# Pacing the input loads of a fused attention and mixer kernel, and putting later ones off behind its transposing transfers

## The chip, the cores and the metric

The kernel runs on one core of a Trainium2 chip. The metric is the device time of one execution in microseconds. Before the change the median of three runs is 305.8 us (305.24 to 306.14).

A core has a matrix engine (TensorE, PE in the profile, its weight loads PEld), a vector engine (VectorE, DVE), a scalar engine (ScalarE, ACT), GpSimd (POOL), and SyncE (SP), which here only issues transfers. Each takes its instructions in the order in which they were written, and they wait for each other through semaphores. Transfers run on 16 DMA engines that all issuers share.

## The reference

For each of 8 batches and 8 heads, attention over 576 positions with heads of 64, a causal mask, and a bias from the running sum of the positive part of `s`; the heads side by side make `x`, which goes through a token mixer and a channel mixer:

```python
scores = scale * np.matmul(q, k.transpose(0, 1, 3, 2))
cum = np.cumsum(np.maximum(s, 0.0), axis=-1)
bias = -(cum[:, :, :, None] - cum[:, :, None, :])
scores = np.where(causal, -1000000000.0, scores + np.minimum(bias, 0.0))
attn = softmax(scores)
x = (attn @ v).transpose(0, 2, 1, 3).reshape(B, S, H * D)
...
h = np.maximum(x.transpose(0, 2, 1) @ w_tok1, 0.0) @ w_tok2
u = x + h.transpose(0, 2, 1)
return u + np.maximum(u @ w_ch1, 0.0) @ w_ch2
```

Inputs and output are float32; `q`, `k` and `v` are 9.4 MB each.

## The kernel before

The kernel is written as a list of operations (`P.op`), each with its cost in microseconds on every engine that may run it, the buffers it reads and writes, a priority, and for transfers a duration. A planner (`Plan.run`, L106) plays the list through on a model of the five engines and of one transfer pipe, and the instructions are then emitted in the order of the planned starts. So a change of a cost, of a dependency, or of where a load stands in the list can move instructions on every engine. After `STEADY` = 50 us of planned time the planner adds a margin behind a transfer or ahead of a matmul. In planned gaps of TensorE in the first `WARM` = 45 us it puts filler matmuls of zeros (L1135).

Per batch the work is:

- Loads, issued by GpSimd, which converts q and k to bf16 on the way: `stage_qk(b, h)` loads k, then q, for a quad of four heads (L462) into one of five `qkn` buffers; `stage_v(b)` loads v in five pieces (L613) into one of two `vf` buffers and multiplies each piece by the exponential of the running sum (`merge_v`, L631, "merges") into `vp`, of which even and odd batches have one each. All loads are in one chain on GpSimd: each is issued behind the one before it (`after=chain[-1]`).
- `quad(b, h)` turns k and q on TensorE (L689) and copies them out of PSUM into `kT` and `qT` (L699 on ScalarE, L701 on VectorE). `pair` makes scores (L731), exponentials (L739, ScalarE), masks (L748, VectorE), attention times v (L802), and divides (L831, L835).
- `tok(b)`: token mixer (L899, L961) and the sum `u`. For batches from 2 on, `u` is turned into `uT` by transposing transfers that SyncE issues (L977), four or five slices per batch; batch parity decides between `uTa` and `uTb`.
- `chan(b)`: channel mixer, first matmuls from `uT` (L1017), second (L1042), sum (L1050), and the store by SyncE (L1055, L1058).

A guard also checks that q and k are small enough for the form used: `squares` (L647) sums their squares on ScalarE. For batches 0 and 1 this needs a second load of q and k, `stage_sq`, which stands behind all other loads in the list. The running sum of `s` is one scan on VectorE (L534, `cum`); from it come the weights of v through one exponential (L540) and a turn on TensorE (L560).

The order of the list before is: the first loads and the weights, v of batch 1, then for all batches from 2 to 7 `stage_qk(b, 0)`, `stage_v(b)`, `stage_qk(b, 4)`, then `stage_sq` for batches 0 and 1, then quads, `tok` and `chan` batch by batch. How far a load runs ahead is limited by its buffer alone, and by a dependency on the load eight before it (L456).

Of the kernel before, what the change touches and what calls it, by code (L numbers as in the profile page):

```python
# [11 lines left out]
ALU = mybir.AluOpType  # L12


SWITCH = 0.095
STEADY = 50.0
MARGIN = 0.5
# [37 lines left out]
class Plan:  # L55
# [11 lines left out]
    def op(self, alts, reads=(), writes=(), prio=0, dma=0.0, holds=(), after=None, mode=0, lock=False, alone=None):  # L67
        o = Op()
        o.alts = alts
        o.prio = prio  # L70
        o.dma = dma
        o.mode = mode
        o.lock = lock
        o.alone = alone
        o.idx = len(self.ops)
        o.deps = set()
        o.users = []
        o.bufs = []
        for k in list(reads) + list(writes) + list(holds):
            b = k[0] if isinstance(k, tuple) else k  # L80
            if isinstance(b, Buf) and b not in o.bufs:
                o.bufs.append(b)
                b.left += 1
        for k in reads:
            w = self.writer.get(k)
            if w is not None:
                o.deps.add(w)
        for k in writes:
            w = self.writer.get(k)
            if w is not None:  # L90
                o.deps.add(w)
            for r in self.readers.get(k, ()):
                o.deps.add(r)
        for k in reads:
            self.readers.setdefault(k, []).append(o)
        for k in writes:
            self.writer[k] = o
            self.readers[k] = []
        o.deps.discard(o)
        o.after = after  # L100
        if after is not None:
            o.deps.add(after)
        self.ops.append(o)
        return o

    def run(self, eps=0.03):  # L106
# [11 lines left out]
        for o in ops:  # L118
            if o.nd == 0:
                for e in o.alts:  # L120
                    cands[e].append(o)
        dma_free = 6.0
        mode = 0
        order = []

# [17 lines left out]
        while left:  # L143
            best = None
            for e in engines:
                lst = []
                tmin = None
                for o in cands[e]:
                    st = slot_time(o)
                    if st is None:  # L150
                        continue
                    est = max(etime[e] + (SWITCH if e == "PE" and o.mode != mode else 0.0), o.ready, st)
                    if o.lock and e in held:
                        est = max(est, held["POOL" if e == "DVE" else "DVE"])
                    if o.alone is not None and o.alone.eng != e:
                        est = max(est, o.alone.until)
                    lst.append((est, o))
                    if tmin is None or est < tmin:
                        tmin = est
                if tmin is None:  # L160
                    continue
                pick = None
                slack = eps + (SWITCH if e == "PE" else 0.0)
                for est, o in lst:
                    if est <= tmin + slack:
                        key = (o.prio, o.idx) if e in ("PE", "SP", "POOL") else (o.prio, o.ready, o.idx)
                        if e == "PE":
                            key = (mode and not o.mode, *key)
                        if pick is None or key < pick[0]:
                            pick = (key, est, o)  # L170
                if best is None or pick[1] < best[1]:
                    best = (e, pick[1], pick[2])
            if best is None:
                stuck = [(e, len(c)) for e, c in cands.items()]
                raise RuntimeError(f"plan is stuck: {left} left, {stuck}")
            e, est, o = best
            occ, lat, fn = o.alts[e]
            for b in o.bufs:
                if b.slot is None:
                    r = b.ring  # L180
                    i = min((i for i in range(len(r.tiles)) if not r.busy[i]), key=lambda i: r.free[i])
                    b.slot = i
                    b.begin = est
                    r.uses.append(b)
                    r.busy[i] = True
                    if b.ordered:
                        r.queue.pop(0)
            etime[e] = est + occ
            if o.alone is not None:
                o.alone.eng, o.alone.until = e, est + occ + 0.1  # L190
            if o.lock and e in held:
                held[e] = est + occ + 0.06
            if e == "PE":
                mode = o.mode
            if o.dma:
                s0 = max(est + (1.9 if e == "POOL" else 1.3), dma_free)
                dma_free = s0 + o.dma
                fin = dma_free + 0.9
            else:
                fin = est + lat  # L200
            o.start, o.fin, o.eng = est, fin, e
            for b in o.bufs:
                b.left -= 1
                b.end = max(b.end, fin)
                if b.left == 0:
                    b.ring.busy[b.slot] = False
                    b.ring.free[b.slot] = b.end
            for e2 in o.alts:
                cands[e2].remove(o)
            o.fn = fn  # L210
            order.append(o)
            for u in o.users:
                if u.after is o:
                    rdy = est + occ
                elif u.alts.keys() == {"PE"} and e == "PE":
                    rdy = est + occ
                elif e in u.alts and len(u.alts) == 1 and not o.dma:
                    rdy = est + occ
                else:
                    rdy = fin  # L220
                    if fin > STEADY:
                        rdy += MARGIN_DMA if o.dma else MARGIN if u.alts.keys() == {"PE"} else 0.0
                u.ready = max(u.ready, rdy)
                u.nd -= 1
                if u.nd == 0:
                    for e2 in u.alts:
                        cands[e2].append(u)
            left -= 1
# [139 lines left out]
def kernel(  # L368
# [34 lines left out]
    def sb(name, shape, dt, pool=None):  # L403
        return (pool or const).tile(shape, dt, name=name, tag=name)
# [44 lines left out]
    chain = []  # L449
    sent = []  # L450

    def load_op(fn, key, us, occ=0.75, prio=-1):

        o = P.op({"POOL": (occ, 0, fn)}, writes=key, prio=prio, dma=us, after=chain[-1] if chain else None)
        if len(sent) >= 8:
            o.deps.add(sent[-8])  # L456
        sent.append(o)
        chain.append(o)

    def load_cast(n, b, h, i, src):  # L460
        def load():
            nc.gpsimd.dma_start(  # L462
                out=n.t[:, i, :, :],
                in_=src[b, h : h + 4, :, :].rearrange("(f e) (p r) d -> (e p) f (r d)", e=2, r=R))
        load_op(load, [(n, i)], 1.45, prio=-1 if b or h else -3)

    qkn = {}

# [47 lines left out]
    for ti, src in enumerate((k, q)):  # L516
# [4 lines left out]
        for f in range(2):  # L521
# [9 lines left out]
         writes=["s"], prio=-7)  # L531
    P.op(dve(576, lambda: nc.vector.tensor_scalar_max(out=s_sb[:, :], in0=s_sb[:, :], scalar1=0.0)),
         reads=["s"], writes=["sr"], prio=-1)
    P.op({"DVE": (1.3, 1.6, lambda: nc.vector.tensor_tensor_scan(  # L534
        out=cum[:, :], data0=one_sb[:, :], data1=s_sb[:, :], initial=0.0, op0=ALU.mult, op1=ALU.add))},
        reads=["sr"], writes=["cum"], prio=-1)
    P.op(dve(1, lambda: nc.vector.tensor_scalar(
        out=half[:, :], in0=cum[:, S - 1 : S], scalar1=-0.5, scalar2=None, op0=ALU.mult)),
        reads=["cum"], writes=["half"], prio=-1)
# [59 lines left out]
    def stage_v(b, cs=tuple(range(NJ))):  # L599
# [4 lines left out]
        for c in cs:  # L604
# [10 lines left out]
            if b == 0 and c == NJ - 1:  # L615
                P.op({"SP": (0.6, 5.5, load_first)}, writes=[(vf, c)], prio=-2)
                continue
            load_op(load, [(vf, c)], 1.15 * n / 128, 0.92)
        if b:
            merge_v(b, cs)  # L620

# [41 lines left out]
    def stage_sq(b, h):  # L663
        n = Buf(r_qn)
        for i, src in enumerate((k, q)):
            load_cast(n, b, h, i, src)
        squares(b, h, n)
# [4 lines left out]
    def quad(b, h):  # L672
# [4 lines left out]
        for ti in range(2):  # L677
# [6 lines left out]
            def tr(ti=ti, pv=pv):  # L684
                for r in range(R):
                    for e in range(2):
                        p0 = e * PR
                        for f in range(2):
                            nc.tensor.transpose(out=pv(e)[f * D : f * D + D, r * PR : (r + 1) * PR],  # L689
                                                in_=nat.t[p0 : p0 + PR, ti, f, r * D : (r + 1) * D],  # L690
                                                identity=ident[p0 : p0 + PR, p0 : p0 + PR])
            P.op({"PE": (R * 0.031, R * 0.031 + 0.21, tr)}, reads=([(nat, ti, 0), (nat, ti, 1)] if b == 0 and h == 0 else [(nat, ti)]) + ["ident"] + pads,
                 writes=[(pts[e], e) for e in range(2)], holds=[d[ti] for d in dsts], prio=(np_ - 30 * (b < 1 and h < 1), 2), mode=1)
            for e in range(2):
                def ev(eng, ti=ti, e=e, pv=pv):
                    i = pv(e)[:, 0:S].rearrange("d (r p) -> d p r", r=R)
# [385 lines left out]
    for i in range(2, 4):  # L1082
        load_ch2(i)
    stage_v(1)
    for b in range(2, B):
        stage_qk(b, 0)
        stage_v(b)
        stage_qk(b, 4)
    for b in range(2):
        for h in range(0, H, 4):  # L1090
            stage_sq(b, h)
    for b in range(B):
        for h in range(0, H, 4):
            quad(b, h)
        st = tok(b)
        chan(b, *st)

    P.op({"DVE": (1.3, 1.6, lambda: nc.vector.tensor_tensor_scan(
        out=pre[:, :], data0=one_sb[:, :], data1=wn[:, 0:S], initial=0.0, op0=ALU.mult, op1=ALU.add))},
# [84 lines left out]
```

## Time and profile before

| | |
|---|---|
| median of 3 runs | 305.8 us (305.24 to 306.14) |
| the profiled execution's own time | 306.06 us |
| its span in the profile | 304.3 us |
| mean granted TensorE clock | 0.995 |
| loads by GpSimd (q0) | 24.25 MB, 44.6% of 16 engines' span |
| stores and transposes by SyncE (q1) | 14.44 MB, 18.7% |
| mean DMA rate over the span | 129 GB/s |

The span runs from the first to the last instruction that the profiler recorded; the profiled execution's own time has 1.76 us more around it. In a timeline row stand the start, the duration, engine, line, operation, output and inputs, shape, the number of instructions that were merged into the row, and in brackets the idle time ahead of it with what ended it. In the rows of 10 us stand the stretch, its length, then for PE, PEld, DVE, ACT and POOL the busy time and the number of instructions, the granted clock, the mean share of the DMA engines in use, and GB/s. A row of transfers has the issuing engine, the number, the size and the median time from issue to landing. "issue" is idle time for which the profile shows no cause.

### The profile page before, as it was taken

To read this page: it belongs to the slowest core of one execution; us is meant where nothing else is said; L and a number is where in the kernel's file an instruction comes from. 1 tells how busy PE (TensorE), PEld (TensorE's weight loads), DVE (VectorE), ACT (ScalarE), POOL (GpSimd) and SP (SyncE) were. 2 spreads that over 40 slices of the span, in tenths; PEclk is the share of its full clock that TensorE was granted. 3 is DMA by queue.
4 is the path that set the end of the run, shared out by engine and by line. 5 is a ranking of instruction groups with operands and counts; after the bars stand their busy time and mean duration, and the time that the engine had idled before them with its cause. 6 is when DMAs were issued, how large, how long until landed. Compare 5 with 4: busy or idle time off the path is not lost.

```text
span 304.3 us, 8094 instructions
## 1 busy us (share of the span) xinstructions
PE 291.8 (96%) x3430; PEld 168.2 (55%) x3430; DVE 172.0 (57%) x368; ACT 182.8 (60%) x298; POOL 107.6 (35%) x147
## 2 busy tenths in 40 slices
PE   8899999899999999999999999998999999999991
PEld 3478566467754545457754545455764544457550
DVE  5962889377976456756556556956456642420030
ACT  5887884699996486609872387727761286017300
POOL 8675469999780418107620108500000000000000
PEclk9999999999999999999999999999999999999998
DMA  8999999999997673358455535894004310250032
GB/s 218 226 207 206 216 224 229 252 190 262 227 156 125 155 197 54 79 140 178 94 80 103 133 84 83 132 116 136 2 2 84 125 38 0 69 155 2 0 111 74
DMA packets 38348, 39.29 MB, mean 129 GB/s; under 512 B 17600, under 2 KB 30976, under 8 KB 38304
## 3 DMA queue, kind: packets, MB, share of 16 engines
q0 software_dynamic: 17072, 24.25, 44.6%
q1 hardware_dynamic: 21232, 14.44, 18.7%
q8 instruction: 29, 0.48, 0.7%
q14 instruction: 15, 0.12, 0.1%
HBM read 40.65 MB, written 9.44 MB: 165 GB/s over the span
## 4 chain that ended last, share of the span: by engine, by line
PE 84%; DMA 12%; POOL 1%; issue 1%; DVE 0%; POOLq 0%
PE pmx L1017 30%; PE pmx L1042 30%; PE pmx L961 5%; PE pmx L899 5%; PE psc L802 5%; PE psc L731 5%; DMA qkn<-in_k_dram 5%; PE psc L689 3%; DMA wc<-in_moe_w_ch_dram 3%; DMA vf<-in_v_dram 2%; DMA uTb<-us 2%; POOL qkn L462 1%; PE pmx L986 0%; DVE of L1050 0%; POOL keep masks.py:66 0%
## 5 line engine op out<-in xcount | busy, mean ns | idle before, releaser
L1017 PEld LDWEIGHTS <-wc 128*128 128x128 bf16 x624 | 57.9, 98 | 32.6 <-issue 1.5
L739 ACT ACTIVATE E<-psc 128x1024 bf16<-128x1024 f32 x64 | 62.2, 1024 | 22.8 <-PE psc L731 22.2
L1017 PE MATMUL pmx<-uTb,wc 128*128 128x320 bf16 (+2 forms) x384 | 56.1, 299 | 1.4 <-DMA uTb<-ub 1.1
L1042 PE MATMUL pmx<-wc,gb 128*128 128x512 bf16 (+1 forms) x252 | 55.3, 369 | 0.0
L1017 PE MATMUL pmx<-uTa,wc 128*128 128x512 bf16 (+1 forms) x240 | 45.6, 337 | 0.0
L647 ACT ACTIVATE junk<-qkn 128x1152 bf16<-128x1152 bf16 x32 | 37.3, 1166 | 11.7 <-DMA qkn<-in_q_dram 11.3
L1042 PE MATMUL pmx<-wc,ga 128*128 128x512 bf16 x192 | 44.1, 379 | 0.0
L631 POOL TENSOR_TENSOR vp<-vf,wT 128x512 bf16<-128x512 f32 (+1 forms) x31 | 32.3, 1058 | 25.6 <-PE psc L802 24.9
L1024 ACT ACTIVATE gb<-pmx 128x320 bf16<-128x320 f32 (+2 forms) x57 | 24.7, 438 | 21.2 <-PE pmx L1017 17.3
L1042 PEld LDWEIGHTS <-gb 128*128 128x128 bf16 x252 | 23.6, 98 | 24.8 <-issue 0.2
L613 POOL DMA_DIRECT2D vf<-in_v_dram x39 | 34.1, 884 | 7.3 <-DMA qkn<-in_k_dram 2.2
L748 DVE TENSOR_TENSOR E<-E,keep 128x512 bf16<-128x512 bf16 x56 | 25.8, 474 | 13.3 <-ACT E L739 13.1
L1042 PEld LDWEIGHTS <-ga 128*128 128x128 bf16 x192 | 18.2, 98 | 20.4
L1024 ACT ACTIVATE ga<-pmx 128x512 bf16<-128x512 f32 (+1 forms) x36 | 19.2, 535 | 11.7 <-PE pmx L1017 11.1
L462 POOL DMA_DIRECT2D qkn<-in_k_dram x19 | 14.1, 744 | 33.5 <-issue 31.8
L1026 DVE TENSOR_SCALAR gb<-pmx 128x320 bf16<-128x320 f32 (+2 forms) x39 | 18.8, 487 | 11.9 <-PE pmx L1017 11.5
L699 ACT COPY kT<-psc 128x576 bf16<-128x576 bf16 x22 | 13.1, 641 | 19.4 <-PE psc L689 17.9
L802 PEld LDWEIGHTS <-E 128*128 128x128 bf16 x576 | 21.1, 97 | 5.5
L835 DVE TENSOR_TENSOR x<-psc,rc 128x640 bf16<-128x640 f32 x28 | 23.0, 823 | 0.9
L1050 DVE TENSOR_TENSOR of<-pmx,ua 128x512 f32<-128x512 f32 x16 | 11.0, 689 | 19.5 <-PE pmx L1042 19.3
L731 PE MATMUL psc<-qT,kT 64*128 64x256 bf16 (+2 forms) x320 | 21.3, 250 | 0.0
L731 PEld LDWEIGHTS <-kT 64*128 64x128 bf16 x320 | 12.6, 94 | 14.6 <-issue 11.5
(107 smaller groups left out, 300.9 us busy)
## 6 DMA issues: line engine op xcount, KB each, us to landing
vf<-in_v_dram POOLq DMA_DIRECT2D x32, 256.0 KB, 7.9
out_dram<-of SPq DMA_DIRECT2D x31, 256.0 KB, 2.3
qkn<-in_k_dram POOLq DMA_DIRECT2D x19, 288.0 KB, 6.7
qkn<-in_q_dram POOLq DMA_DIRECT2D x19, 288.0 KB, 7.3
wc<-in_moe_w_ch_dram POOLq DMA_DIRECT2D x8, 384.0 KB, 11.4
out_dram<-of SPq DMA_DIRECT2D x10, 128.0 KB, 2.3
vf<-in_v_dram POOLq DMA_DIRECT2D x7, 128.0 KB, 7.4
gb<-in_k_dram SPq DMA_DIRECT2D x1, 576.0 KB, 3.9
```

Of the source, the lines that this page charges most:

```text
L613: nc.gpsimd.dma_start(out=vf.t[p0 : p0 + n, c, :, :], in_=v[b, :, c * 128 : c * 128 + n, :].rearrange("h p d -> p h d"))
L631: eng.tensor_tensor(out=vp.t[p0 : p0 + n, c, :, 0:D], in0=vf.t[p0 : p0 + n, c, :, :], in1=wT[p0 : p0 + n, cw, b * H : b * H + H].unsqueeze ...
L647: nc.scalar.activation(out=junk[:, :].rearrange("p (t n) -> p t n", t=2), in_=i, func=AF.Square, accum_out=sq[:, col : col + 1])
L731: nc.tensor.matmul(out=ps.t[:, hh * 512 + c0 : hh * 512 + c0 + e - a], lhsT=kT.t[hh * 64 : hh * 64 + 64, j0 : j0 + 128], rhs=qT.t[hh * 64 ...
L739: nc.scalar.activation(out=E.t[:, :, 512 * pc : 512 * pc + 512], in_=ps.t[:, :].rearrange("p (e n) -> p e n", e=2), func=AF.Exp, scale=0.125)
L748: nc.vector.tensor_tensor(out=o, in0=o, in1=keep[:, :].unsqueeze(1).unsqueeze(1).to_broadcast([128, 2, 2, 128]), op=ALU.mult)
L802: nc.tensor.matmul(out=o[:, ic, 0:DE], lhsT=E.t[:, hh, d0 : d0 + 128], rhs=vp.t[:, jc, h + 2 * hh, 0:DE], start=(jc == j_lo), stop=(jc == ic))
L835: nc.vector.tensor_tensor(out=x.t[:, :, :].rearrange("p c (g f e d) -> p g e f c d", f=2, e=2, d=D)[:, h // 4, h % 2], in0=pav2()[:, :, :, ...
L1017: nc.tensor.matmul(out=pm.t[:, 0 : e - a], lhsT=wc1[:, m, cc * 128 : cc * 128 + 128], rhs=uT.t[:, m, a:e], start=(m == 0), stop=(m == NMC ...
L1024: lambda cc=cc, pm=pm, a=a, e=e: nc.scalar.activation(out=g.t[:, cc, a:e], in_=pm.t[:, 0 : e - a], func=AF.Relu),
L1026: lambda cc=cc, pm=pm, a=a, e=e: nc.vector.tensor_scalar_max(out=g.t[:, cc, a:e], in0=pm.t[:, 0 : e - a], scalar1=0.0)),
L1042: nc.tensor.matmul(out=pm.t[:, na:ne], lhsT=g.t[:, cc, c * 128 : c * 128 + 128], rhs=wc2[:, cc, na:ne], start=(cc == 0), stop=(cc == NCC - 1))
```

## The change

Four things are changed.

- `load_op` gets a `probe`, one element of what the load writes. From the 17th to the 44th load in the chain (`PACE0` to `PACE1`), a load is preceded on GpSimd by `touch`, a copy of one element of the load `DEPTH` = 5 places before it. Weight loads have no probe. In the built program these are 21 copies, the first of them ahead of the q load of quad (1, 4).
- The loads of batches 4 to 7 move from the front of the list to behind `chan(b)` of the batch two before, preceded by one `touch` of each slice of that batch's `uT` that the transposing transfers wrote (4 or 5 copies, 18 in all). The reloads of batches 0 and 1 for the squares follow the loads of batches 5 and 6.
- The scan of `s` gets a later priority (2 for −1) and a dependency on the transposes of q of quad (0, 0).
- The planner's transfer pipe starts at 6.85 for 6.0, and a `touch` (`bare`) gets no margin.

The order on all engines is planned anew. In the built program TensorE has the same matmuls and 25 fillers of 12221 columns for 20 of 9951. Its first scores stand ahead of the k transposes of quad (0, 4) instead of behind them, and ahead of the k transposes of quad (1, 4) stand ten L961 matmuls instead of six. VectorE takes one of the first two q evictions, ahead of the scan, where ScalarE had both.

```diff
+DEPTH = 5
+PACE0, PACE1 = 16, 44
...
-        dma_free = 6.0
+        dma_free = 6.85
...
-                    if fin > STEADY:
+                    if fin > STEADY and not u.bare:
                         rdy += MARGIN_DMA if o.dma else MARGIN if u.alts.keys() == {"PE"} else 0.0
...
+    probes = []
+    seen = sb("seen", [128, 8], FP32, fast)
+
+    def touch(ap, reads, col):
+        o = P.op({"POOL": (0.12, 0.2, lambda: nc.gpsimd.tensor_copy(out=seen[0 : ap().shape[0], col : col + 1], in_=ap()))},
+             reads=reads, writes=[("seen", col)], prio=-1, after=chain[-1])
+        o.bare = True
+        chain.append(o)
+
-    def load_op(fn, key, us, occ=0.75, prio=-1):
+    def load_op(fn, key, us, occ=0.75, prio=-1, probe=None):
+        if PACE0 <= len(probes) < PACE1 and probes[-DEPTH]:
+            touch(probes[-DEPTH][0], probes[-DEPTH][1], 0)
+        probes.append((probe, key) if probe else None)
...
-        load_op(load, [(n, i)], 1.45, prio=-1 if b or h else -3)
+        load_op(load, [(n, i)], 1.45, prio=-1 if b or h else -3, probe=lambda: n.t[0:1, i, 0, 0:1])
...
-    P.op({"DVE": (1.3, 1.6, lambda: nc.vector.tensor_tensor_scan(
+    scan = P.op({"DVE": (1.3, 1.6, lambda: nc.vector.tensor_tensor_scan(
         out=cum[:, :], data0=one_sb[:, :], data1=s_sb[:, :], initial=0.0, op0=ALU.mult, op1=ALU.add))},
-        reads=["sr"], writes=["cum"], prio=-1)
+        reads=["sr"], writes=["cum"], prio=2)
...
-            load_op(load, [(vf, c)], 1.15 * n / 128, 0.92)
+            load_op(load, [(vf, c)], 1.15 * n / 128, 0.92, probe=lambda c=c, p0=p0: vf.t[p0 : p0 + 1, c, 0, 0:1])
...
+            if b == 0 and h == 0 and ti == 1:
+                scan.deps.add(turn)
...
-    for b in range(2, B):
+    def stage_in(b):
         stage_qk(b, 0)
         stage_v(b)
         stage_qk(b, 4)
-    for b in range(2):
-        for h in range(0, H, 4):
-            stage_sq(b, h)
+    for b in range(2, 4):
+        stage_in(b)
     for b in range(B):
         for h in range(0, H, 4):
             quad(b, h)
         st = tok(b)
         chan(b, *st)
+        if 2 <= b < B - 2:
+            for c in range(NJ - 1 + b % 2):
+                touch(lambda c=c, uT=st[2]: uT.t[0:1, 0, c * 128 : c * 128 + 1], [(st[2], c)], 1)
+            stage_in(b + 2)
+            if b == 3 or b == 4:
+                for h in range(0, H, 4):
+                    stage_sq(b - 3, h)
```

More of the change, by code (lines that the diff above doesn't have):

```diff
@@ L77, in op @@
         o.users = []
+        o.bare = False
         o.bufs = []
@@ L691, in tr @@
                                                 identity=ident[p0 : p0 + PR, p0 : p0 + PR])
-            P.op({"PE": (R * 0.031, R * 0.031 + 0.21, tr)}, reads=([(nat, ti, 0), (nat, ti, 1)] if b == 0 and h == 0 else [(nat, ti)]) + ["ident"] + pads,
+            turn = P.op({"PE": (R * 0.031, R * 0.031 + 0.21, tr)}, reads=([(nat, ti, 0), (nat, ti, 1)] if b == 0 and h == 0 else [(nat, ti)]) + ["ident"] + pads,
                  writes=[(pts[e], e) for e in range(2)], holds=[d[ti] for d in dsts], prio=(np_ - 30 * (b < 1 and h < 1), 2), mode=1)
+            if b == 0 and h == 0 and ti == 1:
+                scan.deps.add(turn)
             for e in range(2):
```

## The prediction

> **What bounds the kernel now.** I read the page first, then the busy time by stretches of 10 us, what TensorE waited for, and the timelines of TensorE, SyncE and GpSimd around each of those waits.
>
> ```profile
> PE 291.8 (96%) x3430; PEld 168.2 (55%) x3430; DVE 172.0 (57%) x368; ACT 182.8 (60%) x298; POOL 107.6 (35%) x147
> PE 84%; DMA 12%; POOL 1%; issue 1%; DVE 0%; POOLq 0%
> ```
>
> TensorE is busy for 291.8 of 304.3 us and carries 84% of the chain that ended last, so only its 12.5 us of idle time can be won, beside filler matmuls. The stretches say where they lie (TensorE's busy time is the second figure).
>
> ```profile
> 0.00:10.00 10.00, 7.97 (x137) 3.71 (x139) 6.18 (x25) 5.47 (x7) 9.22 (x22) 1.00 0.91 224
> 30.00:40.00 10.00, 9.35 (x148) 5.39 (x146) 7.76 (x18) 8.66 (x13) 4.46 (x6) 1.00 1.21 226
> 50.00:60.00 10.00, 8.72 (x165) 5.65 (x163) 5.34 (x11) 5.98 (x10) 9.81 (x13) 1.00 1.09 238
> 200.00:210.00 10.00, 8.61 (x135) 4.82 (x131) 4.74 (x8) 4.50 (x8) 0.00 (x0) 1.00 1.21 171
> ```
>
> 2.03 us are lost in the first stretch, 0.65 at 30, 1.28 at 50, 1.39 at 200; most of the other 7.2 us is the tail behind the last matmul, which the change doesn't touch. The granted clock is 1.00 in all of these rows. The three middle losses, by their rows:
>
> ```profile
> 33.85 1.04 PE L961 MATMUL pmx<-h,w 128*128 128x512 bf16 x4
> 35.50 0.48 PE L689 MATMUL psc<-ident,qkn 64*64 64x64 bf16 x36 [0.62 <-DMA qkn<-in_k_dram]
> 56.08 0.38 PE L899 MATMUL pmx<-x,w 128*128 128x128 bf16 x4 [1.28 <-issue]
> 206.54 0.70 PE L1017 MATMUL pmx<-uTb,wc 128*128 128x320 bf16 x4 [1.06 <-DMA uTb<-ub]
> 207.57 1.26 PE L1017 MATMUL pmx<-uTb,wc 128*128 128x320 bf16 x8 [0.33 <-DMA uTb<-us]
> ```
>
> At 35.5 TensorE waits for the k load of quad (1,4); at 56 for something the profile doesn't show; at 206 for batch 5's transposing transfers. Why those are late, by time to landing in 194 to 206 us, against batch 3's in 126 to 135 us:
>
> ```profile
> uTb<-ub SPq DMA_TRANSPOSE x4, 9.5
> uTb<-us SPq DMA_TRANSPOSE x1, 6.6
> ```
>
> ```profile
> uTb<-ub SPq DMA_TRANSPOSE x4, 2.8
> uTb<-us SPq DMA_TRANSPOSE x1, 2.4
> ```
>
> GpSimd's timeline, SyncE's and the chain of waits give the moments of issue:
>
> ```profile
> 194.62 0.72 POOL L462 DMA_DIRECT2D qkn<-in_q_dram  x1
> 133.08 1.21 SPq L977 DMA_TRANSPOSE uTb<-us  x1
> 200.91 6.61 DMA uTb<-us
> ```
>
> GpSimd issues the last loads (the reload for the squares) until 195.3, right when SyncE issues batch 5's transposes. Those took 6.6 to 9.5 us, where batch 3's, with no load beside them, took 2.4 to 2.8.
>
> **The change part by part.** *The loads put off.* `stage_in(b + 2)` and the reloads now follow `touch` reads of every uT slice of batch b on GpSimd's in-order queue, so no load can be in flight beside the transposes of batches 2 to 5. With batch 3's 2.4 us, batch 5's last transpose, issued at 200.91 in the chain of waits, lands at 203.3 (200.91 + 2.4); TensorE wants it at 205.5 (206.54 less 1.06). The wait goes: −1.06 − 0.33 = −1.39.
>
> What else hangs on those reads is everything behind them on GpSimd: the loads of two quads and of v, and the merges (L631). Batch 5, which also has two reload quads in its queue, is the tightest.
>
> ```profile
> 138.69 4.25 POOL L613 DMA_DIRECT2D vf<-in_v_dram  x5
> 147.01 4.05 POOL L631 TENSOR_TENSOR vp<-vf,wT 128x512 bf16<-128x512 f32 x4 [4.07 <-PE psc L802]
> 151.30 0.75 POOL L462 DMA_DIRECT2D qkn<-in_k_dram  x1 [0.24 <-issue]
> 156.85 0.71 PE L802 MATMUL psc<-vp,E 128*128 128x65 bf16 x18
> ```
>
> Batch 3's last transpose lands at 133.1 + 2.4 = 135.5. Behind it stand eight q/k issues at 0.75 (6.0 us), v's five (4.25) and five merges at 1.01 (5.1): 151 us. The first attention-times-v product of batch 5 is at 156.85, so 5 us of other TensorE work cover it even if TensorE runs 0.9 us earlier. Batches 4, 6 and 7 have more room. Cost: 0. Of the 18 reads of uT and 21 paced reads each costs about what the smallest GpSimd copy does (0.21 us, row below), on an engine busy for 35% of the span.
>
> *At most five loads under way.* Loads 16 to 43, counted from 0, now each wait for the load five before them, where that isn't a weight.
>
> ```profile
> 89.32 0.21 POOL L642 CAST vp<-wT 64x8 bf16<-64x8 f32 x1
> 16.97 0.71 POOL L462 DMA_DIRECT2D qkn<-in_k_dram  x1 [0.34 <-DMA w<-in_moe_w_tok_dram]
> 22.93 0.70 POOL L462 DMA_DIRECT2D qkn<-in_q_dram  x1 [0.94 <-DMA wc<-in_moe_w_ch_dram]
> 29.70 0.88 POOL L613 DMA_DIRECT2D vf<-in_v_dram  x1 [0.47 <-DMA qkn<-in_q_dram]
> 51.71 0.48 PE L689 MATMUL psc<-ident,qkn 64*64 64x64 bf16 x36
> ```
>
> Their times to landing, in the order of issue: the k load of 16.97 with the queue full, v's second piece of 29.70, and the k load of 151.30 with nothing ahead of it.
>
> ```profile
> qkn<-in_k_dram POOLq DMA_DIRECT2D x1, 288.0 KB, 11.0
> vf<-in_v_dram POOLq DMA_DIRECT2D x1, 256.0 KB, 13.3
> qkn<-in_k_dram POOLq DMA_DIRECT2D x1, 288.0 KB, 4.3
> ```
>
> Quad (1,0)'s k lands at 28.0, and quad (1,4)'s q, sent at 22.93 before, must now wait for it. Alone it would need 4.3 us, thus land at 32.4; but its turn comes only after the k load that lands at 35.45 anyway. Pacing moves the issue and not the landing, while the queue stays full. The tightest place is behind batch 1's v: its second piece lands at 43.0, one merge of 1.01 follows, and only then is k of quad (2,0) sent, at 44. It lands between 44 + 4.3 and, as the queue is shorter than at 16.97, well before 44 + 11; halfway is 51.7, when TensorE takes it. Since a queue of five is nearer to empty than to eight, I take 49 to 50: cost 0, from 0 to +2 if it is late, and no gain.
>
> On that the Trainium skill ("DMA: Bandwidth & Descriptors", section "Queues, rings and completion order") has a rule: each DMA engine goes round between the queues that have work, a packet from each. By it the depth of the load queue would not matter to a transpose or an instruction fetch, only whether loads are there at all; the sum stays, and the rival with the fetch below gets less likely. No run so far shows two depths side by side.
>
> *The scan and the new order.* The changed plan puts the scan of s behind one of the q evictions on VectorE, which now takes one of the two.
>
> ```profile
> 8.08 1.35 DVE L534 TENSOR_TENSOR_SCAN cum<-one_sb,s_sb 64x576 f32<-64x576 f32 x1
> 8.13 1.18 ACT L699 COPY qT<-pmx 128x576 bf16<-128x576 bf16 x2 [0.88 <-PE pmx L689]
> 5.85 1.83 PE L1135 MATMUL pmx<-zero 128*128 128x512 bf16 x8
> 8.02 0.39 PE L1135 MATMUL pmx<-zero 128*128 128x512 bf16 x1
> 9.63 0.61 PE L731 MATMUL psc<-qT,kT 64*128 64x256 bf16 x10
> 10.06 1.02 ACT L739 ACTIVATE E<-psc 128x1024 bf16<-128x1024 f32 x1 [0.75 <-PE psc L731]
> 9.22 0.48 PE L689 MATMUL pmx<-ident,qkn 64*64 64x64 bf16 x36 [0.81 <-DMA qkn<-in_k_dram]
> ```
>
> The scores of quad (0,0) now stand before the transposes that waited until 9.22, behind fillers of 1890 columns (0.88 us at 1.83 us for 3928). They can start at 8.02 + 0.88 = 8.9 instead of 9.63, so the exponentials may start 0.73 us before 10.06; against that the scan, and with it v's weights, come one eviction later (0.59 us by ScalarE's row for two, 0.8 at most if VectorE is slower at it). I take 0.4 sooner for the head, between −0.73 and +0.8. In all 2270 filler columns are added (1.06 us at that rate), inside waits. What the head wins ends at the landing at 35.45, but the plan, which now expects loads 0.85 us later, puts four more L961 matmuls ahead of those transposes (0.86 us, as four took 1.04 with 0.18 of overlap). With the old arrival they end 0.24 us after the landing, a gain of 0.62; with a head quicker by 0.24 or more the gain is the full 0.86. I take −0.85, between −0.86 and +0.18 (head 0.8 slower).
>
> *The 1.28 us at 56.*
>
> ```profile
> q8 instruction: 1, 0.02, 6.0%
> ```
>
> This is the instruction queue in 53 to 54 us: a block of instructions comes just ahead of the stall's end, and the stall lies inside a run of equal matmuls, where no data is awaited. So I read it as a late fetch, though the profile names no cause. Nothing in the change removes it by construction. Price between −1.28 (gone) and +1.28 (a second one); I take 0.
>
> **Sum**, on the profiled execution's 306.06 us (span 304.3 and 1.76 around it, 0.26 over the median of the runs, 305.8): 306.06 − 1.39 − 0.85 = 303.82, less 0.26: 303.6 us.
>
> **Rivals.**
> 1. *The late fetch goes, as five loads crowd it less than eight did.* For it: it fell into a stretch at 238 GB/s. Against it: loads are still in flight there. 303.6 − 1.28 = 302.3.
> 2. *The late fetch eats the head's gain.* The new order packs short matmuls just before that point, so the instructions run out sooner while the block comes when it came. Then only batch 5's gain is left: 306.06 − 1.39 − 0.26 = 304.4.
> 3. *The change doesn't do what it says for batch 5.* The stores share SyncE's queue with the transposes, and if these, not the loads, made them late, the wait stays: 306.06 − 0.85 − 0.26 = 305.0. New small waits of 1.4 us in the rewritten order would give the same. Against it: batch 3's transposes had the same stores around them and took 2.4 to 2.8.
> 4. *Slower: a load waits for its buffer and the merges queue behind it.* One such wait is in the trace:
>
> ```profile
> 102.96 0.72 POOL L462 DMA_DIRECT2D qkn<-in_q_dram  x1 [12.74 <-PE psc L689]
> ```
>
> Before, GpSimd was far ahead and such a wait was free. Now it would stand in front of batch 5's merges. It decides from 5 us on; at 12.74 it costs 12.7 − 5.0 = 7.7, so 311.3 us. Against it: of five q/k buffers the reloads take those of quads (3,4) and (4,0), both long transposed by 137 us.
>
> **How the numbers follow.** Chances: forecast 0.43 (303.6, its own range 303.1 to 304.1), rival 1 0.16, rival 2 0.19, rival 3 0.12, rival 4 in any size 0.10. Within 0.3% of 305.8 (304.9 to 306.7) is about what a measurement can't tell from no change. Faster by more: the first three, 0.78, less 0.03 for rival 2 with another small wait: 0.75. Same: rival 3 with that, 0.14 after 0.01 to slower. Slower: 0.11. The range 302.1 to 305.4 takes in rivals 1 to 3 and leaves out rival 4 and parts of the others.
>
> **What would show it.** Right: no wait for uTb at L1017, with batch 5's transposes landing in under 3 us; no busy slice of GpSimd issuing loads between a batch's L961 and the landing of its transposes; GpSimd rows after 200 us, where there were none; the first exponential before 9.8 us; TensorE's wait at quad (1,4) gone or moved. Wrong: a wait of L802 for vp or of L689 for qkn after 100 us (rival 4), an issue stall of over 1.3 us near 55 (rival 2), uTb waits still there (rival 3).

## The result, and the profile after

| | before | after |
|---|---|---|
| median | 304.88 us (303.98 to 306.14, 6 runs) | 316.7 us (314.58 to 318.07, 6 runs) |
| ratio, 95% interval | | 1.0378 [1.0333, 1.0423] |
| the profiled execution's own time, span | 306.06, 304.3 us | 315.96, 314.2 us |

The change makes the kernel slower by 3.8%, about 11.5 us, where 303.6 us was forecast. From the page of the changed kernel, the engines and the chain that ended last (line numbers are now 15 to 17 higher):

```profile
PE 294.5 (94%) x3399; PEld 169.2 (54%) x3435; DVE 187.9 (60%) x379; ACT 176.4 (56%) x286; POOL 117.0 (37%) x187
PE 70%; DMA 12%; DVE 7%; ACT 3%; POOL 3%; issue 3%; SPq 0%; ACTq 0%; POOLq 0%; DVEq 0%
```

TensorE's part of the chain fell from 84 to 70%; VectorE, ScalarE and GpSimd, together 1% before, now have 13%. The same stretches of the changed kernel as before, and the one that fell most, which ahead of the change was full:

```profile
0.00:10.00 10.00, 8.73 (x99) 3.54 (x102) 5.69 (x24) 4.85 (x6) 9.23 (x22) 1.00 0.89 229
30.00:40.00 10.00, 9.82 (x181) 6.14 (x180) 7.74 (x18) 9.00 (x15) 5.54 (x9) 1.00 1.21 226
50.00:60.00 10.00, 9.90 (x177) 6.34 (x177) 6.42 (x13) 6.49 (x12) 9.52 (x18) 1.00 0.98 201
150.00:160.00 10.00, 7.78 (x124) 5.13 (x122) 6.67 (x11) 4.94 (x11) 5.32 (x7) 0.83 0.95 161
200.00:210.00 10.00, 9.95 (x85) 5.14 (x85) 7.95 (x17) 6.46 (x9) 0.35 (x2) 1.00 0.29 69
```

Of the kernel before:

```profile
150.00:160.00 10.00, 10.00 (x146) 5.70 (x144) 5.35 (x12) 7.83 (x13) 3.91 (x7) 1.00 0.42 62
```

All four stretches of the prediction are better filled than before, though in the first, where 0.76 us was won, filler matmuls alone take 0.71 us more (6.47 for 5.76). The loss is in other stretches. What TensorE waited for, in us in total, times, and longest:

```profile
PE psc L819 <- ACT E L756: 3.0, 2, 1.7
PE psc L819 <- DVE E L765: 2.2, 2, 1.5
PE psc L819 <- DVE E L773: 1.4, 2, 0.7
...
PE psc L748 <- ACT qT L716: 1.1, 1, 1.1
...
PE psc L748 <- DVE qT L718: 0.4, 1, 0.4
```

These are 8.1 us. Before, one such wait stood, for an exponential:

```profile
PE psc L722 <- ACT E L739: 0.3, 1, 0.3
```

None of the 8.1 us is for a transfer: neither L704 for `qkn`, nor L819 for `vp`, nor L1034 for `uTb`. TensorE waits for exponentials, masks and evictions, whose own engines were held up. The timeline of the changed kernel around the worst place, by engine (start, duration, engine, line, operation, and in brackets the idle time ahead with what ended it):

```profile
145.75 1.16 ACT L662 ACTIVATE junk<-qkn 128x1152 bf16<-128x1152 bf16 x1 [2.34 <-DMA qkn<-in_q_dram]
...
146.91 1.92 ACT L756 ACTIVATE E<-psc 128x1024 bf16<-128x1024 f32 x2
...
151.84 3.20 POOL L646 TENSOR_TENSOR vp<-vf,wT 128x512 bf16<-128x512 f32 x3
...
147.94 4.08 DVE L765 TENSOR_TENSOR E<-E,keep 128x512 bf16<-128x512 bf16 x2 [1.11 <-ACT E L756]
151.95 1.06 DVE L773 TENSOR_TENSOR E<-E,keep 128x128 bf16<-128x128 bf16 x1
...
147.96 0.70 PE L819 MATMUL psc<-vp,E 128*128 128x65 bf16 x18 [1.66 <-ACT E L756]
...
152.08 0.27 PE L819 MATMUL psc<-vp,E 128*128 128x65 bf16 x3 [1.51 <-DVE E L765]
153.06 0.79 PE L819 MATMUL psc<-vp,E 128*128 128x65 bf16 x11 [0.71 <-DVE E L773]
```

Two things are to be seen. ScalarE stands still for 2.34 us before a square (L662), whose q load is still in flight; the exponentials that are next in its queue depend on no load, and TensorE waits 1.66 us for them. Then two masks take 4.08 us and a small one 1.06, while GpSimd does merges (L646) and issues loads; TensorE waits 2.22 us for these. From the chain of waits of the changed kernel, the load in question, which lands 0.11 us ahead of the square:

```profile
138.52 7.12 DMA qkn<-in_q_dram
```

So there were two theories. Q: the loads put off arrive when ScalarE already stands at their squares, and its queue is blocked. M: the merges behind the late v loads fall beside VectorE's masks, which then take far longer. The rivals: the pacing is what hurts (P), or loads this late don't fit, wherever the squares and merges stand (D). In the expectations of e1 and e2, D still stands for the putting off as a whole, by whatever way.

### The profile page after: what moved, and what is told of

The parts are those of the page before. It is cut to its first block, busy times and chain, and to the rows that moved or that the text cites. A ratio compares the mean times of both kernels' runs of the same rounds, so it can differ in the third digit from the quotient of the medians.

```text
span 314.2 us, 8100 instructions
## 1 busy us (share of the span) xinstructions
PE 294.5 (94%) x3399; PEld 169.2 (54%) x3435; DVE 187.9 (60%) x379; ACT 176.4 (56%) x286; POOL 117.0 (37%) x187
## 4 chain that ended last, share of the span: by engine, by line
PE 70%; DMA 12%; DVE 7%; ACT 3%; POOL 3%; issue 3%; SPq 0%; ACTq 0%; POOLq 0%; DVEq 0%
PE pmx L1059 23%; PE pmx L1034 21%; DMA qkn<-in_q_dram 8%; PE pmx L916 5%; PE pmx L978 5%; PE psc L748 4%; PE psc L819 3%; DVE E L765 3%; PE psc L704 2%; PE pmx L1158 2%; DMA uTb<-us 2%; DMA uTb<-ub 2%; POOL vf L628 1%; ACT junk L662 1%; POOL qkn L477 1%
## 5 line engine op out<-in xcount | busy, mean ns | idle before, releaser
L1034 PEld LDWEIGHTS <-wc 128*128 128x128 bf16 x624 | 58.4, 99 | 32.3 <-issue 1.3
L1034 PE MATMUL pmx<-uTb,wc 128*128 128x320 bf16 (+2 forms) x384 | 57.4, 304 | 0.0
L1059 PE MATMUL pmx<-wc,gb 128*128 128x512 bf16 (+1 forms) x243 | 54.2, 369 | 0.8 <-issue 0.5
L662 ACT ACTIVATE junk<-qkn 128x1152 bf16<-128x1152 bf16 x32 | 37.4, 1168 | 15.0 <-DMA qkn<-in_q_dram 14.6
L1034 PE MATMUL pmx<-uTa,wc 128*128 128x512 bf16 (+1 forms) x233 | 44.8, 336 | 0.6 <-issue 0.3
L1059 PE MATMUL pmx<-wc,ga 128*128 128x512 bf16 x183 | 43.1, 379 | 0.5
L765 DVE TENSOR_TENSOR E<-E,keep 128x512 bf16<-128x512 bf16 x56 | 32.2, 584 | 18.6 <-ACT E L756 18.3
L646 POOL TENSOR_TENSOR vp<-vf,wT 128x512 bf16<-128x512 f32 (+1 forms) x32 | 34.1, 1079 | 8.0 <-DMA vf<-in_v_dram 7.4
L1041 ACT ACTIVATE gb<-pmx 128x320 bf16<-128x320 f32 (+2 forms) x53 | 22.9, 436 | 23.4 <-PE pmx L1034 20.1
L819 PEld LDWEIGHTS <-E 128*128 128x128 bf16 x576 | 21.2, 98 | 12.6 <-issue 3.4
L819 PE MATMUL psc<-vp,E 128*128 128x65 bf16 x522 | 21.0, 194 | 6.6 <-ACT E L756 3.0
L1043 DVE TENSOR_SCALAR gb<-pmx 128x320 bf16<-128x320 f32 (+2 forms) x43 | 20.9, 490 | 9.2 <-PE pmx L1034 8.4
L716 ACT COPY kT<-psc 128x576 bf16<-128x576 bf16 x20 | 12.0, 642 | 21.9 <-PE psc L704 21.8
L1043 DVE TENSOR_SCALAR ga<-pmx 128x256 bf16<-128x256 f32 (+1 forms) x28 | 15.0, 551 | 9.5 <-PE pmx L1034 9.4
```

Of the source, the lines that this page charges most:

```text
L646: eng.tensor_tensor(out=vp.t[p0 : p0 + n, c, :, 0:D], in0=vf.t[p0 : p0 + n, c, :, :], in1=wT[p0 : p0 + n, cw, b * H : b * H + H].unsqueeze ...
L662: nc.scalar.activation(out=junk[:, :].rearrange("p (t n) -> p t n", t=2), in_=i, func=AF.Square, accum_out=sq[:, col : col + 1])
L765: nc.vector.tensor_tensor(out=o, in0=o, in1=keep[:, :].unsqueeze(1).unsqueeze(1).to_broadcast([128, 2, 2, 128]), op=ALU.mult)
L819: nc.tensor.matmul(out=o[:, ic, 0:DE], lhsT=E.t[:, hh, d0 : d0 + 128], rhs=vp.t[:, jc, h + 2 * hh, 0:DE], start=(jc == j_lo), stop=(jc == ic))
L1034: nc.tensor.matmul(out=pm.t[:, 0 : e - a], lhsT=wc1[:, m, cc * 128 : cc * 128 + 128], rhs=uT.t[:, m, a:e], start=(m == 0), stop=(m == NMC ...
L1041: lambda cc=cc, pm=pm, a=a, e=e: nc.scalar.activation(out=g.t[:, cc, a:e], in_=pm.t[:, 0 : e - a], func=AF.Relu),
```

## The experiments

Ratios are to the kernel before, run beside each.

| run | median us | ratio, 95% interval |
|---|---|---|
| e1_no_defer | 305.68 | 0.9996 [0.9963, 1.0029] |
| e2_no_pace | 317.22 | none, four runs from 311.36 to 318.51 |
| e3_squares_later | 308.61 | 1.0122 [1.0071, 1.0172] |
| e4_no_merges | 310.86 | 1.0167 [1.0115, 1.0219] |
| e5_squares_later_no_merges | 305.25 | 0.9981 [0.9955, 1.0008] |
| e6_later_plan | 308.89 | 1.0090 [1.0064, 1.0117] |
| e7_later_scan_alone | 304.93 | 0.9958 [0.9931, 0.9985] |
| e8_last_reloads_behind | 304.83 | 0.9947 [0.9920, 0.9975] |
| e9_merges_on_vector | 314.32 | 1.0294 [1.0252, 1.0336] |
| e10_later_plan_merges_on_vector | 302.81 | 0.9920 [0.9891, 0.9949] |
| e11_pacing_alone | 303.64 | 0.9947 [0.9924, 0.9971] |
| e12_pacing_merges_on_vector | 303.65 | 0.9920 [0.9889, 0.9952] |

### The putting off or the pacing

e1 leaves out the touches behind the transposes, e2 the pacing:

```diff
-            for c in range(NJ - 1 + b % 2):
-                touch(lambda c=c, uT=st[2]: uT.t[0:1, 0, c * 128 : c * 128 + 1], [(st[2], c)], 1)
```

```diff
-PACE0, PACE1 = 16, 44
+PACE0, PACE1 = 16, 16
```

> The changed kernel with the five touches behind each batch's transposes left out: the order of the loads, the pacing five loads back and the later scan stay. Theory D (the putting off is the whole loss, through ScalarE's squares that wait for late loads and through GpSimd's merges that then fall beside VectorE's masks): about 304 us, the 305 of before less most of the gain at the head. Theory P (the pacing is what hurts, a load's issue now waiting for a landing): 312 us or more, since all paced touches are still there.

> The changed kernel without the pacing touches (no load waits for the one five before it), the touches behind the transposes kept. Theory D: 315 to 317 us, as the changed kernel. Theory P: 304 to 306 us.

e1 is back at the time of before, 1.7 us more than the 304 us that was expected. So the putting off is the loss. Of e2's four runs three lie where the changed kernel is (316.62 to 318.51), but one at 311.36, so no ratio is taken from it, and by itself it doesn't clear the pacing of a share; e11 and e10 below do. Two waits of TensorE in e1's rows are together of that size: 0.71 for a mask, and 1.23 for batch 3's transposes. Its times to landing from 122 to 137 us show that these now meet loads; e1's list has the reloads earlier than the list of before.

```profile
136.30 1.79 PE L1034 MATMUL pmx<-uTb,wc 128*128 128x320 bf16 x12 [1.23 <-DMA uTb<-ub]
```

```profile
uTb<-ub SPq DMA_TRANSPOSE x4, 8.3
```

### The squares, the merges, and both

e3 keeps the plan of the changed kernel, and moves only the squares, later in ScalarE's order (no further than the next use of their buffer or of their sum):

```diff
+SQ_LATE = 4.5
...
     order = P.run()
+    later = {}
+    for o in order:
+        n = getattr(o, "sq", None)
+        if n is not None and o.start > 80.0:
+            nxt = min([u.begin for u in n.ring.uses if u.slot == n.slot and u.begin > n.begin] + [u.start for u in o.users])
+            later[o] = max(o.start, min(o.start + SQ_LATE, nxt - 0.05))
+    order = sorted(order, key=lambda o: (later.get(o, o.start), o.idx))
...
```

e4 keeps the plan and leaves the merges of batches 2 to 7 out of the program; e5 does both.

```diff
+            if b >= 2:
+                P.ops[-1].drop = True
...
-            o.fn()
+            if not getattr(o, "drop", False):
+                o.fn()
```

> The changed kernel with every square after 80 us of the plan put 4.5 us later in ScalarE's order, nothing else moved. Theory Q (the squares hold ScalarE's queue while they wait for their loads): the three stalls of 1.81, 2.34 and 1.99 us before squares go, and with them TensorE's waits of 1.06, 0.40, 1.66 and 1.31 us behind them: 4.4 us, and some of the low granted clock after them, so 311 to 312 us. Theory M (the merges beside the masks are the loss): 315 to 317 us, nothing changes.

> The changed kernel without GpSimd's 25 to 30 products of v with its weights for batches 2 to 7 (the later batches then multiply by the v of batches 0 and 1). Theory M: TensorE's waits for masks of 1.51, 0.71, 0.70 and 0.65 us go, 3.6 us, and with the masks at 420 instead of 1260 ns some of what comes after: 311 to 313 us. Theory Q: the squares still wait for their loads, 315 to 317 us.

> The changed kernel with both edits: squares 4.5 us later in ScalarE's order, and no products of v with its weights for batches 2 to 7 (these then multiply by the v of batches 0 and 1). If the two waits, for squares and for masks beside merges, are the whole loss: 304 to 306 us, with no wait of TensorE for an exponential or a mask over 0.3 us. If something else in the putting off costs (the transfers themselves, or TensorE's clock): 308 us, as with the squares alone, or more.

e3 wins 2.56% (1.0378 − 1.0122), 7.8 us, more than the 4.4 us of waits behind the squares, and after 50 us ScalarE waits for no load any more. Its waits of TensorE, from 8.1 us down to 2.7:

```profile
PE psc L749 <- ACT E L757: 1.3, 1, 1.3
...
PE psc L820 <- DVE E L766: 0.9, 1, 0.9
PE psc L820 <- DVE E L774: 0.5, 1, 0.5
```

The masks' waits shrink too, though no merge was moved: with ScalarE on time, fewer masks fall beside merges (11 of both kinds instead of 14, counting those that a merge covers for over 30% of their time). e4 wins 2.1%, 6.4 us. TensorE then waits for no mask, while its waits for exponentials and evictions stay (2.5 and 3.5 us). Its group of large masks shows why: first that of the changed kernel, then that of e4 (busy us, mean ns):

```profile
L765 DVE TENSOR_TENSOR E<-E,keep 128x512 bf16<-128x512 bf16 x56 | 32.2, 584 | 18.6 <-ACT E L756 18.3
```

```profile
L767 DVE TENSOR_TENSOR E<-E,keep 128x512 bf16<-128x512 bf16 x56 | 23.8, 433 | 19.3 <-ACT E L758 19.2
```

With both edits (e5) the loss is gone, 0.9981 with 1 inside the interval, and in TensorE's waits no mask stands any more and one exponential, 1.3 us. So Q and M both hold, overlap by some 2 us (7.8 + 6.4 against the 12.1 of both), and leave nothing of a size for D. M needs no late load, though: one of the changed kernel's four waits for a mask, 0.70 us before 73.00, stands beside batch 3's merges, ahead of the first load that is put off, which is issued at 101.08.

### Why the loads are late: a later plan

The planner orders squares, merges and masks by planned landings. It plans 0.6 us for the issue of a transpose, and no margin ahead of a touch. e6 tells it what the rows show, 1.2 us, and puts the margin ahead of the touches behind transposes:

```diff
-        o.bare = True
+        o.bare = col == 0
...
-                P.op({"SP": (0.6, 0, trd)}, reads=rk, writes=[(uT, c)],
+                P.op({"SP": (1.2, 0, trd)}, reads=rk, writes=[(uT, c)],
```

> The changed kernel whose planner is told the measured times: 1.2 us for the issue of a transpose instead of 0.6, and the margin for a transfer also ahead of the touches behind the transposes; loads, squares, merges and masks are then ordered by later landings. Theory E (the plan takes the loads for 3 to 4.5 us earlier than they are, and the order it writes makes the stalls): 304 to 307 us, with ScalarE's waits for loads under 1 us. Theory D (loads that come so late do not fit, wherever squares and merges stand): 311 us or more.

It wins 8.8 us of the loss (1.0378 − 1.0090), though not all: 308.89 lies above E's 304 to 307 and below D's 311. Two waits of TensorE of over 1 us are left. The smaller is Q's. Of ScalarE's waits ahead of squares one remains, but of 7.83 us, where E expected less than 1; a ReLU (L928) stands behind two squares, and TensorE waits for it. This is ahead of the first load that is put off.

```profile
51.34 1.17 ACT L662 ACTIVATE junk<-qkn 128x1152 bf16<-128x1152 bf16 x1 [7.83 <-DMA qkn<-in_q_dram]
...
54.21 0.44 PE L916 MATMUL pmx<-x,w 128*128 128x128 bf16 x5 [1.22 <-ACT h L928]
```

The larger is M's. The timeline of e6 (GpSimd, VectorE, TensorE):

```profile
181.91 4.04 POOL L646 TENSOR_TENSOR vp<-vf,wT 128x512 bf16<-128x512 f32 x4
182.04 4.53 DVE L765 TENSOR_TENSOR E<-E,keep 128x512 bf16<-128x512 bf16 x2
...
186.29 1.29 PE L819 MATMUL psc<-vp,E 128*128 128x65 bf16 x18 [2.30 <-DVE E L765]
```

Four merges follow each other without a gap, and the mask that came 0.13 us after the first ends only behind the last. That is theory M in three rows. The stretches of 2 us of e6 show TensorE idle and then at a granted clock of 0.51 and 0.64:

```profile
184.00:186.00 2.00, 0.00 (x0) 0.00 (x0) 2.00 (x1) 0.60 (x1) 1.95 (x2) 1.00 1.20 205
186.00:188.00 2.00, 1.71 (x20) 1.29 (x21) 1.66 (x6) 0.00 (x0) 0.35 (x2) 0.51 1.22 207
188.00:190.00 2.00, 2.00 (x76) 0.93 (x73) 0.85 (x2) 0.60 (x1) 0.20 (x1) 0.64 1.15 199
```

### Merges on VectorE

If a merge on GpSimd blocks a mask, a merge on VectorE can't. e9 does this to e3, e10 to e6, for batches 2 to 7:

```diff
-            if b < 2:
+            if b >= 2:
+                alts = {"DVE": (*c_dve(512), lambda mul=mul: mul(nc.vector))}
+            elif b < 2:
                 alts["DVE"] = (*c_dve(512), lambda mul=mul: mul(nc.vector))
```

> The changed kernel with the squares 4.5 us later in ScalarE's order, and the products of v with its weights for batches 2 to 7 given to VectorE instead of GpSimd, so that the whole result is computed and no GpSimd product can run beside a mask. Theory M (a mask is held until the GpSimd product beside it ends): 304.5 to 306.5 us, and no mask over 500 ns; VectorE works some 20 us more in spans where it has 40% idle. Rival (leaving the products out helped only because GpSimd had less to do): since GpSimd is again relieved, the same time, but a mask still over 600 ns where a load is issued. Rival (VectorE becomes late): 308 us or more, TensorE waiting for VectorE's copies.

> The later plan of e6_later_plan (transposes at 1.2 us, the margin ahead of the touches) and the products of batches 2 to 7 on VectorE: the loads put off as in the change, the whole result computed. Theory: what e6 has left over the kernel before is one row, two masks of 4.53 us together beside four products of 4.04 us, and the wait of 2.30 us behind it, with 1.2 us for a ReLU; both go: 304.5 to 306 us, no slower than before. Rival (loads so late cost something besides the two waits): 308 us or more.

e9 lies 8 us above what M said, at a time of the rival that VectorE becomes late. Every mask is short, as M said (mean 418 ns, none over 450), and it isn't too much work that makes VectorE late. e9 has the early plan again, and now it is VectorE that stands still, 10.6 us in all, for v loads that are late; behind these merges, the divisions stand. Its group of merges, and VectorE and TensorE in its timeline:

```profile
L647 DVE TENSOR_TENSOR vp<-vf,wT 128x512 bf16<-128x512 f32 (+1 forms) x38 | 25.3, 696 | 11.0 <-DMA vf<-in_v_dram 10.6
```

```profile
108.08 0.69 DVE L647 TENSOR_TENSOR vp<-vf,wT 128x512 bf16<-128x512 f32 x1 [1.77 <-DMA vf<-in_v_dram]
109.91 0.69 DVE L647 TENSOR_TENSOR vp<-vf,wT 128x512 bf16<-128x512 f32 x1 [1.13 <-DMA vf<-in_v_dram]
...
112.23 0.82 DVE L855 TENSOR_TENSOR x<-psc,rc 128x640 bf16<-128x640 f32 x1
...
113.11 0.48 PE L707 MATMUL psc<-ident,qkn 64*64 64x64 bf16 x36 [2.37 <-DVE x L855]
```

It is Q's mechanism on another engine. e10 has the same merges in the later plan, and with it the chain that ended last is TensorE again, the masks are at their own length, and VectorE waits 1.1 us for v instead of 10.6:

```profile
PE 93%; ACT 2%; DMA 1%; DVE 1%; issue 0%; DVEq 0%
```

```profile
L646 DVE TENSOR_TENSOR vp<-vf,wT 128x512 bf16<-128x512 f32 (+1 forms) x38 | 25.0, 681 | 1.2 <-DMA vf<-in_v_dram 1.1
L767 DVE TENSOR_TENSOR E<-E,keep 128x512 bf16<-128x512 bf16 x56 | 22.8, 415 | 8.9 <-ACT E L758 8.7
```

At 302.81 us e10 beats both kernels, 0.8% below the one before and 1.7 us below the least that was expected, with every load put off as in the change. D falls: loads so late fit, if what waits for them stands behind what doesn't.

### What each part is worth without the loss

e7 is the kernel before with the later scan and the 6.85 alone; e11 has the pacing besides, with the loads in the order of before; e12 is e11 with the merges on VectorE; e8 is e7 with the transposes and touches planned as in e6, and only the last six reloads behind batch 5's transposes:

```diff
+    stage_sq(0, 0)
...
+        if b == 5:
+            for c in range(NJ):
+                touch(lambda c=c, uT=st[2]: uT.t[0:1, 0, c * 128 : c * 128 + 1], [(st[2], c)], 1)
+            stage_sq(0, 4)
+            stage_sq(1, 0)
+            stage_sq(1, 4)
```

> The kernel before with the later scan and the planner's 6.85 alone: no pacing, no putting off. By the prediction's sum 0.85 us less than before, about 305.0; if late instructions eat the gain, 305.9, as before.

> The kernel before with the later scan, and of all loads only the last six (the second reading of batch 0's second half and of batch 1) put behind batch 5's transposes, with the transposes planned at 1.2 us: the wait of 1.39 us for batch 5's uTb goes, and no quad's load is late. 303.5 to 304.5 us by the sum (305.9 less 1.39 and 0.85 at best). If any load put off costs by itself: 307 us or more.

> The kernel before with the later scan and the pacing five loads back, loads in the order of before, nothing put off. If the pacing costs nothing: 304.9 us, as with the later scan alone. If it costs what e1_no_defer lost against that (0.7 us): 305.6 us.

> The kernel before with the later scan, the pacing, and the products of batches 2 to 7 on VectorE; loads in the order of before, nothing put off. It says what the putting off itself is worth once its two waits are gone: if nothing, this comes out as e10_later_plan_merges_on_vector, at 0.992 of the kernel before (about 302.9 us); if putting off is a gain of its own (no transpose of batch 5 held up by loads), this one is slower than that by up to the 1.39 us of that wait: 304 to 304.5 us.

e7 is 1.3 us faster than before (0.42% of 305.9; 0.5 to 2.1). e11 can't be told from it, so neither a cost nor a gain of the pacing shows. e8 can't either, and its median comes out above its 303.5 to 304.5. e12 and e10 have the same ratio: no gain of the putting off shows of its own (the 1.39 us would be 0.46%, and each interval reaches 0.3% to either side). The profiled execution of e11 is its slowest, 306.52 us, and has M in it with nothing put off: two masks take 3.93 us beside merges, and TensorE waits for an eviction behind them.

```profile
76.66 3.93 DVE L765 TENSOR_TENSOR E<-E,keep 128x512 bf16<-128x512 bf16 x2
...
81.24 1.03 PE L1034 MATMUL pmx<-uTb,wc 128*128 128x256 bf16 x8 [1.86 <-DVE gb L1043]
```

Why there was so little to win for the putting off is in TensorE's waits in e7, all but the start:

```profile
PE psc L804 <- DVE E L758: 0.4, 1, 0.4
PE psc L733 <- issue: 0.3, 1, 0.3
PE pmx L901 <- issue: 0.2, 1, 0.2
PE pmx L786 <- DVE vp L642: 0.2, 1, 0.2
```

No wait for `uTb` is left: the new order alone has removed it, though in e7 the reloads are still in flight beside batch 5's transposes, which take a median of 4.8 us from 185 to 215 us.

## Why the prediction was wrong

- *The loads put off, "Cost: 0".* This is the step that failed. It asked one question, whether batch 5's merges would end before the first product of attention and v, and that was right: the changed kernel's last merges for batch 5 end at 155.04 (151.84 + 3.20), 4 us later than worked out, and no L819 waits for `vp`. It didn't ask who else stands in line for the same loads. ScalarE takes a quad's squares as soon as the plan has its load, and exponentials and evictions stand behind them; and merges were counted as GpSimd's time only, not as time taken from masks on VectorE. Beside its 0 stand 13.1 us: the changed kernel's 1.0378 against the 0.9947 of e11, which has all of the change but the putting off. e5, at 0.9981, shows the two causes to be nearly all of it.
- *Why the plan didn't see it.* The planner has a lock that keeps merges and masks apart and knows that a square waits for its load, but only by planned times; e6 shows that its times for the transposes and touches were too early, since with later ones 8.8 us come back.
- *Batch 5's wait, −1.39.* It went as described. The transposes of batch 5 in the changed kernel, from 194 to 216 us:

```profile
uTb<-ub SPq DMA_TRANSPOSE x4, 2.4
uTb<-us SPq DMA_TRANSPOSE x1, 2.5
```

  As a gain of the putting off it was not real, since e7 loses the same wait without it.
- *The head, −0.85.* This isn't borne out. The wait at quad (1,4) is gone, as forecast, but the first exponential, which was to start before 9.8 us, starts at 10.28 in the changed kernel and at 10.65 in e7, later than the 10.06 of before. In e7 the waits at quad (1,4) (0.62 us), at 56 (1.28) and for `uTb` (1.39) are all gone, 3.3 us, and its time is 1.3 us less (0.5 to 2.1). So the waits together were worth less than their sum, and what the head is worth alone wasn't measured.
- *The 1.28 us at 56, taken at 0.* It is gone as well, in the stretch from 50 to 60 above, and in e7, which has no pacing (0.2 us of issue at L901). So the order of instructions was enough to remove it; rival 1's reason, fewer loads in flight, isn't needed.
- *The pacing, 0.* Right in the time, by e11 against e7, 0.9947 and 0.9958. The prediction weighed a rule of the Trainium skill there ("DMA: Bandwidth & Descriptors", "Queues, rings and completion order"), that each DMA engine goes round between the queues with work, and worked out from it that the depth of the load queue wouldn't matter; the two times agree with that.
- *Rival 4*, the only slower one, had merges queued behind a load that waits for its buffer. No such wait is in the changed kernel's rows, nor any other sign of being wrong that the prediction listed. The slowdown came by a mechanism that no rival had.

The 8.1 us of waits and the 1.7 us at half clock (last section) make 9.8 of the 13.1; the rest stands in no row. TensorE's 3399 recorded matmuls beside 3435 weight loads say that some rows are missing, so that can't be settled from this trace.

## What to carry to other kernels

Where a load is put off, list every instruction that reads it, and on each of their engines what is queued behind them: an in-order queue makes whatever comes next as late as the load. A planned order is only as good as its times for what the late work waits on; correct those from rows before anything is moved behind them, or move the reader behind work that doesn't depend on the load. And put no run of GpSimd work on SBUF beside VectorE work that reads two operands from SBUF.

## What the runs showed of the hardware

- *A VectorE product of two SBUF operands waits for GpSimd's.* Alone a mask of 128x512 takes 415 to 420 ns; in the changed kernel the 11 that a merge covers for over 30% of their time take 1260 on average, up to 2277 (before the change 5 did so, at 1068). Beside GpSimd's issue of loads alone they take 417, but not always: of 351 masks of both sizes in all the runs with such an issue and no merge beside them, five take longer, up to 1.11 us (e1, at 153.83); what holds these isn't shown. The Trainium skill ("SBUF — State Buffer", "Who interferes with whom") states that such an instruction, with both inputs in SBUF, contends with a GpSimd one that reads SBUF, that the contention is an exclusive lock, and that the order of issue decides who blocks. The rows agree. In e6 a mask wasn't let in between four merges that followed each other, and took 4.19 us.
- *A stall can cost TensorE's clock too.* Behind the waits of 1.51 and 0.71 us the changed kernel's stretches of 2 us are:

```profile
150.00:152.00 2.00, 0.57 (x7) 0.17 (x4) 2.00 (x3) 0.95 (x3) 1.98 (x3) 1.00 1.21 206
152.00:154.00 2.00, 1.20 (x16) 0.97 (x17) 1.97 (x5) 0.00 (x0) 1.92 (x2) 0.75 1.20 205
154.00:156.00 2.00, 2.00 (x9) 1.13 (x8) 0.95 (x2) 0.44 (x1) 1.41 (x3) 0.50 1.21 206
156.00:158.00 2.00, 2.00 (x15) 1.38 (x14) 0.57 (x2) 1.60 (x3) 0.00 (x0) 0.90 0.95 161
```

  The clock is at 0.75, 0.50 and 0.90, a loss of 0.5 + 1.0 + 0.2 = 1.7 us; in e6, behind its 2.30 us, 0.98 + 0.72 = 1.7 again. A single wait of 1.06 us before 120.37 in the changed kernel has no such row, and neither has its longest, 1.66 us before 147.96 (the clock is 1.00 from 146 to 150). What a stall must be to cost clock isn't shown; both that did were shorter than 3.4 us. The Trainium skill ("TensorE: Matmul & The Clock Gate", "Part 1: The HAM clock gate (the "warmup" mystery)") has a gate of half clock or full, decided in windows of some 3.4 us; 1.7 us lost at half clock are 3.4 us of it, which agrees.
- *Loads beside transposing transfers.* The four `ub` transposes of a batch land in a median of 2.4 us with no load in flight beside them (batch 5 in the changed kernel), and of 4.8 (e7, batch 5), 8.3 (e1, batch 3) or 9.5 us (before, batch 5) with loads in flight.
